# A new order table, searched with a price for each change of TensorE's tile shape

## The chip, the cores and the metric

The kernel runs on one core of one Trainium2 chip. The metric is device time in microseconds (us) of one execution. Five engines matter: PE (TensorE, matrix multiply), DVE (VectorE), ACT (ScalarE), POOL (GpSimd) and SP (SyncE, which here only issues DMAs). Each engine works through its own queue in order and waits on semaphores for the others.

## The reference

Two independent layers, whose outputs are put side by side (L = 2048, D = 576):

```
A:  K = 2 Re( sum_n C[d,n] exp(A[d,n] dt[d] l) )      (d = 576, n = 128, l = 2048)
    y = causal convolution of u with K (by FFT of length 4096) + u * D_skip
B:  q, k, v = x @ wqkv          (32 heads of 18)
    phi(z) = [softmax(z w_phi), softmax(-z w_phi)]
    o = phi(q) (phi(k)^T v) / (phi(q) sum phi(k) + 1e-6);   out = o @ wo
out = concat(A, B)              (2048 x 1152, float32)
```

## The kernel before, in words

The function `body` doesn't issue instructions. It records 2902 operations through `Plan.op` (engine, planned cost, dependences, buffers, and for PE a tile shape `mode`), and `Plan.run` then issues them in the order of the table `ORDER`. The table is the only thing that sets the order on every queue. An entry is the number of an operation; `*` says that the operation goes to its second engine (a copy listed as ACT may go to DVE, a product listed as POOL may go to DVE, or the other way round), `/3` names the buffer slot that a tile gets (8 PSUM slots `ps`, 14 large ones, 19 row ones, 7 small ones), and `+12` puts twelve dummy matmuls on zeros (line 227) ahead of a PE operation.

```
            x, *slots = x.split("/")
            x, _, fill = x.partition("+")
            second, k = x.endswith("*"), int(x.rstrip("*"))
```

The work falls into units. The helpers `mm` (line 447), `copy` (452 to 457) and `tt` (462 and 466) issue most of it, so lines alone say little; the tiles' names do:

- **fold**: w_phi is multiplied into the weights, `ps<-fT,e`; the result is split in a high and a low half, `wh` and `wl`.
- **key** (16 tiles of 128 tokens): three products of 14 matmuls each with `wh` and `wl`; the two softmaxes (`small`, `e`: on DVE maxima, minima and `e<-ps,small`; then `e<-small,e`, the exponential on ACT (592), pair sums `o<-e` on POOL (595), and the scaling `e<-e,small` and `v<-v,small`); then the state phi(k)^T v, `ps<-e,v`, 32 small products in 128x32 tiles. The sixteenth of these ends the first stage of the kernel.
- **query** (16 tiles): a product, softmax, transposes (697), `ps<-kvb,fT`, transposes (726), the output product, `ot`.
- **u** (16): the first step of u's transform, `ps<-kb,w`, in 32x64 tiles, copied to `zi`.
- **group** (18, two halves each): the kernel K by powers. Phases are added on POOL (899), cosines and sines come from ACT (909 to 917), exponents from PE (`ps<-sel,mg`) and ACT (933), the factors `E` and `cs` from DVE (944, 948, 950) with some on POOL, and `ps<-E,cs` on PE in 128x32 tiles. The last of its 36 halves ends the second stage.
- **kfirst**, **product**, **last**: the other steps of the transform: `ps<-ks,w` in 32x128, `ps<-ub,ff` in 64x32 and `ps<-kb,ff`, `ps<-ac,ff` in 32x32, `ps<-zi,w` in 128x64 tiles, with copies out of PSUM to `zi`, `us`, `zo`, `yo`, 288 wide.

Of the 486 PE operations 336 use the whole 128x128 array, 150 a smaller tile shape.

Of the kernel before, what the change touches and what calls it, by code (L numbers as in the profile page):

```python
# [277 lines left out]
0/0 2 1 3 261/0 4/1 153/2 234/3 374/4 33 396/5 12/1 72/6 288/7 19/8 1363 1362 40/2 46/0 375/3  # L278
1360 5/4 369/9 1361 26/5 376 1249/10 1329 377* 13+26/0 15 266/11 16 35/1 20/2 1368 1367 1369/12 1371 1370
1372 14/3 17 22 21/4 38 34/5 1373 18 41 1374 1379 36 23 1167 50/13 1250*/14 47 42 1331/6  # L280
48 1375 1364 39 1376 24 1365/0 1377 1518 25 1366 7+32/6 1378 1380 1381/15 1519 10 11 6/7 8
1289/16 9 27+2/0 1332/7 37 1382 1333/8 29 1251 1383 28/3 31 379+2/2 212/17 1384 30 1349/18 1330 1385 43/9
267/10 1252/1/4/6/7/11 131/4 32 1386 1523 1256 1387 1388 268* 269* 1253 1255 1516 382/0 380/5 1353/8 1199/12 239/1 1334
1335 1179/15 397 1291/10 383 1517 51/12 1341/1 1389 1390 1475/0 1336 271/0 1290 482 384/13 1309/14 1239/11 1337 1524
52* 1342 213/0 53 1476 1525/16 385 1292/3/7/1/6/1 1477 1168 1338 272/2 1296 1293 1254 1258/0 347/10 1257 386 1478
1344 1295 44 1527 270/0 388*/1 387 1479 55/6 274/2 1294 1339 278 389 1297 56/3 132/4 45 1351/13 1480
57/4 58/3 59 1535 60/5 275 1354 276/2 390 277 1340 1520 1481 1201/8 381/1 1200 391/12 1521/1 62 1699
1522 61 63 73 1350 1343 64*/4 65 1526 1345 158/18 279 214* 240/6 273/7 215 218/5 74 398 133*
392/5 280*/6 1346 393/0 66 67/17 1347 1348 289 1298 241* 54/1 394 1484 1482 1352 1202/6/0/3/4/8 1528 1209/12 242
223/1 217/1 1205 68/3 1204 1206 290 281* 1483 395 399 69/4 245/2 224 225/9 70* 1203 1529 1391/0 1392  # L290
1434/1 1435 348/11 1207 219/3 1241/8 221 1485 1436 1698 75* 1437 1530 1531 220 222 235 1438 1439 1490/0/10/7
1532 483 1533 1700 236* 282 1503/4/1/12 1488/7 1505/6 251/2 1486/5 1491 49/1 401/13 1548/1 246/3 71 1489 1219/1 226*/5
250 216/2 1493 283/17 1494 1208 1487 1506 1534 76 400 1440 227 1299/16 243/3 1492 1547 284/6 134 228
285/0 252/5 1279/6 244/0 263 229/4 1536 1701 1705 1537/17 1210/5 262 1504 1495 1355 1496 137/5 230/3 1538 104/4
286* 1539 455/17 1441 1442 1240* 248 231/4 1501/3 428/11 1540 287 143/1 1510 1356 247 1541 1497/2/13/0 154 232
1542 378/4 136/7 349* 253/5 1511 350 1702 1502 1498 249 135/5 138/4 254 1319/10 1509 1706 1507 237 255
1508 1512/0 1543 233 142 140 155 144/8 139 1242/3/6/4/5/6 256/8 351/6 291* 402/7 1513 1499 238 141 1246 320/3
429/10 1544 1545 1245 1244* 1243 1248 292 1269/7 1447/5/3/1 352/4 159/12 145*/6 1357 1443 1444 430* 257/3 293/8 258/2
431 353/3 1546 1221/11 146 1220 355/5 1707/1 356 1549/0 432/7 1247 1550 1551 1445/7 354/6 1552 1500 1553 359
1554 1717 358 147 1446 370 361/4 357/4 1709 1449/2 435/4 371 1451 1448 1450 360 1514 1515 362 105/9  # L300
1555 160* 1454 434/6 1452 363 1211 148/12 1453 1212/7/3/0/2/2 1455 1358 321/6 1214* 161 1456/5 450/5 364/18 452 1216
# [12 lines left out]
1421/4 1729/0 469/2 1415/3 1425 1422 470 184 1424 1169/15 421 426 1429 191/5 1128/4 1416 1601/0/7/5 1724 1730 113/3
471 1428 1427 472/2 1417 208 1603/2 1426 1430/4 1899 1604 112 1725 114/11 422 111/7 1884 473/5 1418 322
196 1600 1726 474/4 197 128 323 324/13 110/6 198 294/1 1889/2 1605/3 1610 1727 1728 1431 207 199*/2 200*
295* 1602 1813/1 475* 1642/5/3/9 480 1606 115 1611 127 1432 1643 1607 1609 1814 325/7 476 201 1815 1644/2
116 1608 328/1 1645 1646/0 427 202/3 1647 1612/3 1649 117 481 1613 1614 118/0 1816 119 1652 327/6 1650
1651 120 1817 1615 1818 1616 1433 1648 1618/0/2/3/4/12 344/1 329 296 78/5 203/6 1621 1819 326/6 204/2 121/12 330/7
297/14 298/5 1620 205* 122/5 210 331 1891 1622 1619* 123/4 1820 1822 1623/1 206 315/8 342 1624/3/7/2/4/2 79* 99/3  # L320
124* 343 299/0 1890 1170/12 1892 332 125* 334/3 301/0 333 129 1628* 1823 300/6 1627 1821 302 316 303/6
304 1626 1617 335 1636/2/4/5/7/13 336 305 1893 306 80* 307*/6 308 1270/2 81/15 1653/0/12/1 337/9 1625 1629 1638 1637*
130 1640 1301/18 338/2 1630/2/3/4/7/3 309 1772/0 1773 1774 1639 1654 1641 317 1655 1633 1828/5/9/11 1632* 1775 1824/6 1826/4
1631* 339/5 1634 1829 1832 1776 83/3 1831 1825 1777 1827 1833 1635 1830 1894 534/0 1778 100 82/7 1779
1834 310/9 89/1 340 345 84/2 1895 311/4 85 1281*/9 1781 341 312/3 1656 88 90/2 86 1780 1280* 1271*
# [12 lines left out]
1678 1668/0 1675 1669 1677 1140/9 1175 1177 1674 1302+13/7/2/6/1/3 632 1909 1679/0 1686 633/10 1141/6 538 1303 1142 1693
1306 1305 1304 1687/7 1143 634/2 1308 1746/1/8/11 1683/6 1911/1 1144 1688 1692 1307 1145+2/2/8 1684 539 1691 1680 1147/4/16
# [811 lines left out]
```

## Time and profile before

| | |
|---|---|
| median of 3 runs | 540.7 us (539.54 to 542.01) |
| span of the profiled execution | 538.2 us |
| PE busy | 519.2 us |
| DVE busy | 455.0 us |
| ACT busy | 412.1 us |
| POOL busy | 332.1 us |

The results give no time of the profiled execution of its own beside the span, which counts from its first to its last instruction; the median of the runs is 2.5 us above it. Sums below are made in the span.

### The profile page before, as it was taken

To read this page: it belongs to the slowest core of one execution; us is meant where nothing else is said; L and a number is where in the kernel's file an instruction comes from. 1 tells how busy PE (TensorE), PEld (TensorE's weight loads), DVE (VectorE), ACT (ScalarE), POOL (GpSimd) and SP (SyncE) were. 2 spreads that over 40 slices of the span, in tenths; PEclk is the share of its full clock that TensorE was granted. 3 is DMA by queue.
4 is the path that set the end of the run, shared out by engine and by line. 5 is a ranking of instruction groups with operands and counts; after the bars stand their busy time and mean duration, and the time that the engine had idled before them with its cause. 6 is when DMAs were issued, how large, how long until landed. Compare 5 with 4: busy or idle time off the path is not lost.

```text
span 538.2 us, 19714 instructions
## 1 busy us (share of the span) xinstructions
PE 519.2 (96%) x8198; PEld 435.3 (81%) x8198; DVE 455.0 (85%) x992; ACT 412.1 (77%) x728; POOL 332.1 (62%) x379
## 2 busy tenths in 40 slices
PE   7899999999999889999998999999999999999996
PEld 6799988999988678798896877876788896777985
DVE  3799998899998888999996999898968669868563
ACT  4699989899879988989898788899796455554432
POOL 1568899977978875975584579768365245223310
PEclk9899999999999999999999999999999999999999
DMA  8898893633426495575397756797466876997687
GB/s 261 290 314 241 282 344 121 213 84 136 142 91 200 120 321 155 146 188 190 94 265 267 247 178 203 229 302 229 149 226 207 253 220 212 306 292 225 203 299 207
DMA packets 77496, 116.41 MB, mean 216 GB/s; under 512 B 9187, under 2 KB 54371, under 8 KB 77407
## 3 DMA queue, kind: packets, MB, share of 16 engines
q1 hardware_dynamic: 77406, 115.16, 67.8%
q8 instruction: 64, 1.05, 0.8%
q14 instruction: 26, 0.20, 0.1%
HBM read 65.87 MB, written 49.26 MB: 214 GB/s over the span
## 4 chain that ended last, share of the span: by engine, by line
PE 73%; DVE 8%; ACT 6%; POOL 6%; DMA 4%; issue 2%; SPq 0%; POOLq 0%; ACTq 0%; DVEq 0%
PE ps L447 68%; PE ps L697 3%; POOL cs L899 3%; DMA ub<-in_u_dram 1%; DMA e<-in_wqT_dram 1%; DMA e<-in_wkT_dram 1%; PE ps L726 1%; DVE cs L944 1%; POOL e L462 1%; DVE ac L466 1%; DMA ff<-in_ff_dram 1%; ACT e L592 1%; POOL E L462 1%; DVE small L584 1%; DVE e L466 1%
## 5 line engine op out<-in xcount | busy, mean ns | idle before, releaser
L447 PE MATMUL ps<-wh,x 128*128 128x288 f32 (+2 forms) x1008 | 242.0, 320 | 2.4 <-ACT wh L513 1.9
L447 PEld LDWEIGHTS ps<-wh,x 128*128 128x128 f32 x1008 | 174.2, 189 | 14.2 <-ACT wh L513 2.2
L447 PE MATMUL ps<-wl,x 128*128 128x288 f32 (+2 forms) x560 | 176.1, 315 | 0.3 <-DVE wl L514 0.3
L447 PEld LDWEIGHTS ps<-wl,x 128*128 128x128 f32 x560 | 106.0, 189 | 1.4 <-DVE wl L514 0.6
L899 POOL TENSOR_TENSOR cs<-cs,pi 128x64 int32<-128x64 int32 (+4 forms) x90 | 92.0, 1022 | 6.1
L595 POOL TENSOR_TENSOR o<-e 128x576 f32<-128x576 f32 x32 | 42.6, 1334 | 33.2 <-ACT e L592 25.7
L462 POOL TENSOR_TENSOR E<-v,cs 128x512 f32<-128x512 f32 x30 | 38.1, 1290 | 28.4 <-ACT v L940 28.3
L466 DVE TENSOR_TENSOR ac<-us,ps 128x576 f32<-128x576 f32 x64 | 44.8, 746 | 6.6 <-PE ps L447 4.8
L462 POOL TENSOR_TENSOR e<-e,small 128x576 f32<-128x576 f32 x31 | 36.7, 1183 | 14.9 <-DVE small L462 13.9
L933 ACT ACTIVATE ps<-ps 128x512 f32<-128x512 f32 x72 | 41.7, 592 | 5.2 <-PE ps L447 4.8
L944 DVE TENSOR_TENSOR cs<-ps,cs 128x1024 f32<-128x1024 f32 x36 | 43.7, 1214 | 2.1 <-ACT ps L933 1.7
L447 PEld LDWEIGHTS ps<-E,cs 128*32 128x32 f32 x2304 | 34.2, 110 | 13.7 <-issue 7.8
L447 PEld LDWEIGHTS ps<-kvb,fT 126*128 126x128 f32 (+1 forms) x320 | 39.1, 189 | 6.5 <-issue 1.9
L447 PE MATMUL ps<-sel,mg 128*128 128x512 f32 x108 | 41.8, 442 | 1.4 <-ACT zi L452 0.4
L447 PE MATMUL ps<-E,cs 128*32 128x64 f32 x2304 | 40.0, 221 | 2.7 <-issue 0.8
L447 PE MATMUL ps<-kvb,fT 126*128 126x133 f32 (+1 forms) x320 | 42.4, 280 | 0.0
L917 ACT ACTIVATE cs<-cs,hp 128x1024 f32<-128x1024 f32 x36 | 40.6, 1143 | 0.0
L592 ACT ACTIVATE e<-e 128x1152 f32<-128x1152 f32 x32 | 37.4, 1168 | 3.6 <-POOL e L462 3.4
L452 ACT ACTIVATE zi<-ps 128x288 f32<-128x288 f32 x91 | 32.2, 414 | 10.2 <-PE ps L447 10.0
L462 POOL TENSOR_TENSOR e<-small,e 128x576 f32<-128x576 f32 x26 | 31.4, 1206 | 10.9 <-DVE e L466 3.9
L909 ACT ACTIVATE cs<-cs 128x2048 f32<-128x2048 int32 x18 | 34.5, 1919 | 3.7 <-POOL cs L899 3.7
L916 ACT ACTIVATE cs<-cs 128x1024 f32<-128x1024 int32 x36 | 36.8, 1054 | 0.3
(145 smaller groups left out, 1056.2 us busy)
## 6 DMA issues: line engine op xcount, KB each, us to landing
dram<-zi SPq DMA_DIRECT2D x32, 288.0 KB
xd<-x SPq DMA_DIRECT2D x16, 576.0 KB
x<-xd SPq DMA_DIRECT2D x16, 576.0 KB
dram<-zi SPq DMA_DIRECT2D x16, 576.0 KB
kb<-dram SPq DMA_DIRECT2D x32, 288.0 KB
ub<-dram SPq DMA_DIRECT2D x32, 288.0 KB
dram<-zo SPq DMA_DIRECT2D x32, 288.0 KB
zi<-dram SPq DMA_DIRECT2D x16, 576.0 KB
```

Of the source, the lines that this page charges most:

```text
L447: pe.matmul(o, l, r, start=start, stop=stop, skip_group_check=skip)
L452: op(("act", "dve"), (c_act(n), c_dve(n)), lambda e: act.activation(dst(), src(), AF.Copy) if e == "act" else dve.tensor_copy(dst(), src() ...
L462: op(eng, [c_dve(n[0]) if e == "dve" else c_pool(n[1]) for e in eng], lambda e: (dve if e == "dve" else pool).tensor_tensor(dst(), a(), b( ...
L466: op(eng, c_dve(n) if eng == "dve" else c_pool(n), lambda: e.tensor_tensor(dst(), a(), b(), op=alu), r=r, w=w, with_=with_, lock=eng == "p ...
L592: op("act", c_act(1152) + 40, lambda: act.activation(e.t, e.t, AF.Exp), r=[e], w=[e], table="exp")
L595: op("pool", c_pool(517), lambda: pool.tensor_tensor(pair.t, e.t[:, :, :, 0:9], e.t[:, :, :, 9:18], op=ALU.add), r=[e], w=[pair], lock=True)
L899: op("pool", c_add(4 * n * W), lambda n=n, j=j: pool.tensor_tensor(x()[:, :, :, n:2 * n], x()[:, :, :, 0:n], pi.t[:, j:j + 2, gs].bitcast( ...
L909: op(("act", "dve"), (c_act(n) + 45, c_dve(n)), lambda e: act.activation(cs.t[:, 0], x(), AF.Abs) if e == "act" else dve.scalar_tensor_ten ...
L916: op("act", c_act(64 * W) + 150, lambda at=at: act.activation(at(1), at(1).bitcast(I32), AF.Sin, scale=TURN), r=[cs], w=[sine], with_=[cs] ...
L917: op("act", c_act(64 * W) + 225, lambda at=at: act.activation(at(0), at(0), AF.Sin, scale=-TURN, bias=hp.t), r=[cs, hp, sine], w=[both], w ...
L933: op("act", c_act(512) + 12, lambda: act.activation(ps.t, ps.t, AF.Exp), r=[ps], w=[ps], table="exp")
L944: op("dve", c_dve(64 * W), lambda: dve.tensor_tensor(F(), both(M.t), F(), op=ALU.mult), r=[M, ready], w=[long], with_=[cs])
```

## The change

Only the table `ORDER` is replaced (one line longer; line numbers behind it rise by one, so that 447 becomes 448). Operations, buffers and arithmetic are the same.

```diff
 ORDER = """
-0/0 2 1 3 261/0 4/1 153/2 234/3 374/4 33 396/5 12/1 72/6 288/7 19/8 1363 1362 40/2 46/0 375/3
...
+2607 1103 2736 836 1104* 2737 2633 2632 2860/0 2861/3/0/16 2895/7 2896/4/5/18 2853/4 2862 2863 837/0/5 2897* 839/6
...
 """.split()
```

Counted in the two tables, in issue order:

| | before | after |
|---|---|---|
| changes of tile shape between successive PE operations | 209 | 187 |
| of these up to the sixteenth key state product | 50 | 42 |
| up to the last of the 36 group products | 161 | 138 |
| dummy matmuls, ahead of so many operations | 94, 10 | 59, 2 |
| operations on DVE | 992 | 1027 |
| operations on ACT | 686 | 637 |
| operations on POOL | 375 | 389 |
| DMAs on SP | 363 | 363 |

The order on every queue is perturbed from end to end, while the sequence of units stays nearly the same. Two places show what moves.

PE's queue in the key stage, before, around a visit to the small tile shapes (`x_529` and `x_737` are the input tiles of two key tiles, `v_95` and `v_107` the values of two others):

```order
L447 MATMUL ps<-wl,x_529 128x396
L447 MATMUL ps<-E,cs 32x64 x32
L447 MATMUL ps<-kb,w_210 64x288 x8
L447 MATMUL ps<-e,v_95 19x36 x32
L447 MATMUL ps<-e,v_107 19x36 x32
L447 MATMUL ps<-sel,mg 128x512
L447 MATMUL ps<-wh,x_737 128x378
```

The same stretch of PE's queue after (`x_519` and `x_960` are input tiles, `v_85`, `v_701`, `v_720` and `v_396` values of four key tiles):

```order
L448 MATMUL ps<-wl,x_519 128x396
L448 MATMUL ps<-e,v_85 19x36 x32
L448 MATMUL ps<-E,cs 32x64 x64
L448 MATMUL ps<-e,v_701 19x36 x32
L448 MATMUL ps<-e,v_720 19x36 x32
L448 MATMUL ps<-e,v_396 19x36 x32
L448 MATMUL ps<-kb,w_256 64x288 x8
L448 MATMUL ps<-wh,x_960 128x378
```

Six operations in 128x32 tiles now stand in one visit; before, this visit held three of them, split by one in 32x64.

POOL's queue before, at the first softmaxes of the key tiles (`e<-small,e` forms the second exponent, `cs<-cs,pi` adds phases for a group):

```order
L899 TENSOR_TENSOR cs<-cs,pi 128x64x8
L462 TENSOR_TENSOR e<-small,e 128x576
L899 TENSOR_TENSOR cs<-cs,pi 128x64x16
L595 TENSOR_TENSOR o<-e 128x576
L462 TENSOR_TENSOR e<-small,e 128x576
L462 TENSOR_TENSOR x_432<-zo,x_432 64x128
```

DVE's queue after, at the first softmaxes of the key tiles:

```order
L467 TENSOR_TENSOR e<-ps,small 128x378
L463 TENSOR_TENSOR kb<-ub 128x288
L463 TENSOR_TENSOR small<-small 128x32
L463 TENSOR_TENSOR kb<-ub 128x288
L463 TENSOR_TENSOR e<-small,e 128x576
L463 TENSOR_TENSOR x_519<-zo,x_519 128x512
L463 TENSOR_TENSOR e<-small,e 128x576
```

Two of the second exponents that stood on POOL now stand on DVE. Over the whole table DVE gains 35 copies of 128x288 out of PSUM from ACT (u 5, kfirst 5, product 10 into `us` and 4 into `zo`, last 5, query 6) and 14 smaller copies; from POOL it gains one `e<-small,e` (four more in the key stage, three fewer in the query stage), three `e<-e,small` and two `v<-v,small`, and it gives up seven `ac<-ac`, three `E<-v,cs` and eleven of the tiny `small<-small`.

Counted along DVE's queue, the last DVE operation that the sixteenth key state product depends on is the 359th before and the 380th after; for the last group product it is the 808th before and the 827th after.

More of the change, by code (lines that the diff above doesn't have):

```diff
@@ new lines @@
+249 1540 1501/5 1502 1507 228 229/13 1503/4 1504 1510 219/7 236 1493 230/0 136/1 246/2 1700 1705 231/1 254 1506 1508
+76 1511 1541 1542 347/9 348/8 1356 140/5 255 1509 1543 232 1357 233 1544 1441 1547/1 1442 153 1443 234 287* 1358 1240
+263 237* 243/5 349* 1211/11 350 139 1207 1545 256/9 428/13 1512/3/5/9 154 1497/4 1498 1499 1500 141/12 143 142 144
+429/13 430* 1219/18 238 292 1221/4 1701 1706 1297 1708 1717 1707/5 431* 400 126/7 145*/1 1208 1242/2/7/5/4/11 1245
+1710 1513* 1246* 146 1243 1514 1244 1444 257/5 353/1 1248 370*/13 1546 1549/1 358/1 1447/7/3/2 1220 1448 359 1445/2
@@ new lines @@
+166 1228 1473 443 168/12 1562/5/2/3 365/4 1299/16 1474 1227 1394 1395 1459 1575/2/7/13 1229/9 1180/6 1579/7 1580 1396
+1563 1570 1702 1564/3 1582 1569 1583 1397 164/4 169 170 1565 444 1699 1576 1567 445/1 408/1 446/1 1560/7 366/5 171
+1577/5 1578 1398 1561 172*/3 1711 1566 1568 173 181 407/6 406/4 413/3 367 368 104/3 456/6 165/3 1585 457* 372* 373
+105/8 447/4 174 458 448* 1261/18 412 1581 1584 1571/2 449 414/1 410 409 1399 411 1400 207/5 1586/5 453 175/13 1587*
+415/4 425 185/8 186/10 182 454 187* 1703/0 1401 1406/4/7/13 1404/3 1408/1 1588 482 1712 1405 1713 1714 176/3 177/1
@@ new lines @@
+121/1 299/7 316 329 330/5 206 1821 298/2 300/3 122/3 210 332 123/5 1627 331 333 334/4 304/2 124 335* 305 306/0 301 129
+336 1617 1636/1/7/4/5/13 1638 302 1637 303 1640 1653/2/12/8 125 1270/1 307*/5 308* 1301/13 1628* 1629 317* 1639* 1641
+337/8 1892 309 338/5 339/2 1884 1772/1 1773 1630/1/3/7/6/6 1632* 1774 1634 1279/12 1824/5/10/9 1775 1654 1655 1825
+340* 1656 1776 1777 1828/4 297/15 1830 1633 1829 1831 1826/6 1827 1834 1631 1833 83/3 100* 310/8 341 88/5
+1262/1/5/7/2/11 1264* 1266* 1894 89 1635 1271* 311/4 312/3 427 1832 82/6 85 1319/18 313 1265* 1263 1267 1268 84/2 1778
@@ new lines @@
+1134 1175* 1907 1908 1909 1135 1137/5 1173* 1136 623/7 1739 628 627 626/13 629 1138 630/2 631 1012/2 1014/4 1668/5
+1670/0 1015 1741 1673 1676 1675 1013/7 1327 1177 1669 1674 1139 1140/16 1302/1/6/4/3/0 1671 1678 1141/3 632
+1683/5/11/5 1684 1306 633/13 1178 1305 1017 1142 1143 1144 538 539 1677 634/3 1016/10 1685/3 1686 1693 1692 1746/4/4/1
+1747 1304 1018 1679/0 635 1020/5 636 1680 2038 1681 637 1019 1682 1145/2/13 1303 1146 1147/6/16 1149/1/0 1148 1687/3
+1688 497 1744/2 540/3 1151/6 1745 1150 1689 541 1742/1 1154/0 1743 642/5/13 643 638/7/0 639 1690 1691 1694/3 640/7/16
@@ new lines @@
+1857 2046 1919 1862/0/1/4/6/11 1864* 1027 1858* 2037 2055 2041/0 2042 1912 1969/2/4/3 2049 2048 1860* 2219 1230/17
+2050 2051 1920 2052 1866 1307 2053 656/3 658* 1855 659 2054 1028/5/2 1865 1863* 1867 2056 1032/7/14 2057/4 1033 2058
+1166 1190/7 2059 2060 2061 2062 1970/10 2218 1973* 701/1 705 706 2220 1965/7 1029* 1030/0/18 1966 1861 1031 708/5
+1967/4 1968 857/3 1972* 1921 1868/5/0/2/6/10 1870 1869 707 1971 709 862/2 861 1872* 1922 1974 863/11 1037/1 1034/7
+1231* 1871 1923 1874/3/5/0/6/0 1038/3 1975 1976/2/2/1 1310* 2222 1035/4 1036/2 1875* 2063 2064 1039 1040/1/3 2065
@@ new lines @@
+1940 2469/17 1924/6 1048 718/3/2 716/7/9 1925 1945 1930 719 935/2 721 725/5 726/4 717 722/1 2001 1935/6 723/0 724/2
+727 2002 2003 1946* 1950/4 870 871 939 940 941 872/5/9 873 1951* 728/1/7 1952 1953 729/0 2470/18 874/2/1 875* 2066
+2069/1 2070 730 2478/13 2449/16 2472/4/5/3/0/2/10 2474* 2475* 2004 2473 2071 1936 878/2 2477/14 731 732 1937
+2479/7/3/5/4/13/8 2221 1938 2535/0 2480 2226 2481 894/9 2476 2483 876/0/9 2005 2482 879/3 2072 2073 880/10 2074 2075
+2491/4 2078 2076 734/6 736*/2 877* 733/3 2223/1 2537/5 735 2227/13 2229 2543/15 2228 2231 2484/2/5/4/7/14/7 2536/12
@@ new lines @@
+2170* 2464* 2500/9 2499/1 910 2501/2/7/4/1/2/4 2465 2257 2466* 2162/0 2163 2505 544/6 2260 2502 2468 2504 2463* 2467
+2258 2503 546/5 2168 547 548/5 2559/5 968/2 2150/7/3/4/1/8 2152* 2151* 970* 2740/12 971 2153* 2169* 2154 2173/0/12/7
+2174* 2149/3 2259 2175 2261 2156/3/1/6/5/9 2160 2264/4/13/1 2558/18 2265 2158* 2176 2159* 911/2/3 912* 596
+2506/5/1/7/0/7/1 2157* 2509* 2262/2 2510 2508 2266/3 2512 2507* 915/0/4 2263 2271 2272 2268 2267/6 2428/1/7/6/5/9/14
+2429* 2333/0 2408/0 2334 2335 2431* 2511 2432* 913/3/15 914* 2336 2337 545/4 549 916 2402/11 2338 550 2339 551 2340
@@ new lines @@
+928/0 609/3 610/7 2688/15 558 2417 2298 2299 2300 930*/9 2560/5/6/7/4/11/0 2563 2561* 2566/8 2301 2564* 2446 2351*
+2352* 2355/0 559 560/5/5 2363/4/9/1 2562* 561 2361/7 2362 2411 2364/17 2366* 2367* 2413 607 2356* 2414 2415 2357 2358
+562/6/18 563 2369 929/1 2418/5/3/2/0/4/16 931 2368 2419 2420* 2421* 2359/6 2360 564/7/6 565 2365 2565/3
+2567/5/1/4/3/0/11 738/6 739/2 2571 2307/3/5/8 2570 2569 2422 2568 2308/17 2311 611/6/0 2661/10 612/10 613 2370/4 2371*
+2372 2373 2177/0 2572/5/1/3/7/11/7 2574* 2302 2573* 566/6 2318/5/0/11 2322/1 2178 2576 2320/7 2179 741/5 2305/4 2180
@@ new lines @@
+2381 2397* 2391 2791/4/2/5 2395* 677/7/13 2398 764/1 765/5 2792* 2793 761/6 766/9 2396 762/0 763 2399 1060 1061
+1062/16 2389 678 2393 2794 2795 779/2 784 783 785 786*/0 787 767/4/6 768/3 769 1063/3 1064 2832/11 679/1/2 770 771
+974/7 978/5 681/4/9 979 682* 980/4 973/2 975 1065 2823 976 680 686/4 687/3 688/9 788 683/7 977 2833/2/4/16 789/17 2834
+790/3 1066 2695/7 2694/15 2696/6/1/3/0/2/5 684/4 685 689/7/5 981/2 982 983 2701 690/11 984/9 2796 2824 2702 691 692
+772/4 2703 774/18 2704 2835 1069/7/11 2836 1070 2660/2 1067/0/7 1068 693 2697 2698 2663/5/4/2/3/15/5 2667 2664* 2665
@@ new lines @@
+2669/17 2666 2668/13 2670/1/0/6/7/6/0 1071/5/4 2699 2700 1072 2671 1073/4 2705/1/5/2/3/13/17 2672 2709 2804/1 2706
+2675 985/4 2676 986 987 791 1089/7 792 2707 2837 2673 793 2838 2812/6/0/7 2580/6 2813 2805/1/3/9 2814 2677 2581/10
+2708 2806* 2815 2807 2808 2741/2/0/7/5/5/16 2742 1076/6 2747/15 2744 2743 1074/3 1075/0 2746/14 2748/7/1/2/3/1/9
+796/4/4 2674 1077/0 1078 2745 2753 2678 694/6 797 2754 2749 2711/2 2755 696/16 2679/7/3/4/2/14/15 2682 2710 2683
+2636/12 2816 2750 2582/1/5/0/6/5/13 2817 794/2/2 2751* 2681* 2752 2586 2809 2680* 2584 795 2756* 2757/7/3/4/6/6/10
@@ new lines @@
+2761 2583* 2587/17 2585* 2758 2588/11 2589/1/5/0/2/0/6 2598 2635/7 2597 2599 2759 2760 988 695/6 2590 697 2591 2592
+2593 2594 2637/0/2/4/3/13/11 2641 2685 798/5/5 799 2595* 2596* 800/6 801/2 2765/1 2639 2600* 2638* 2684 2640 803/4
+804/0 2601/2/5/3/1/2/14 2605 2602 2762 2603 989/0/4 802/5 2642/17 2604 805 990 2643/15 2644/6/7/4/1/0/6 2645 806/5/2
+2763 2766/7 2646 807/12 808 2647 2650 2648 773/3 809 775 810 2764/12 2767/5/7/6/0/13/5 2768 2771 2649 2651* 2652
+2772/6 2773/3 698 2770* 2774/2/3/1/4/3/11 2779 2780 2781 2769 2776 991/5/11 992 2775 2714/10 811/7 813/5 2712/15
@@ new lines @@
+2713/17 2810 776 2653/3/4/5/1/3/6 2655 2782 2654 2715/2/6/0/7/13/16 2717* 2718 993/3/18 2719 2716* 995/4 2657* 996/0
+997/4 2721/1 2720/7 2722/1/2/7/6/4/0 2728 994 998/3 2608/9 2656 2727 2724 999/0 2777 2778 2617/8 2723 2729 1000 2730
+812/4 814 2783/2/7/6/5/16/11 2787* 2609/10 2784 2785* 2610/17 2786 2725 2611/3/1/0/4/13/18 2615* 2726 2616/1
+2618/7/6/5/2/3/11 2613 2612 1001/4/1 1002/12 2614 2620 816/6 818/3 2619 2624 2731/0/7/6/2/13/4 2735 2732 2621 2734
+2622 2733 1003 2623 2625* 2789 2658 2788 822/0 817/4 2626* 820 819 2627/7/6/0/5/16/18 2606 1090/2 2629 1004 1005 2631*
@@ L424 @@
+1117 1118/2/6 1119/6 1010 1120 2854/4/7/4 2855* 2856 1121 1122 2875/0/3/9 2881/7 2876 2857 2868/7/2/0 2858 2877 2869
+2889/3/6/16 2901 2878 2880 2890* 2891 2879 2847/0/2/13 2870 2871 2848 2872 2882/6/4/5 2873 2883 1124/2 2859 2849 851/4
+2892 2894 2884 2885 2886 852/6 2850 2893 853* 2851 2887 1126*/0 854 1123/0 2852 1125 1127
 """.split()
```

228 lines of the change are left out of this document (83 added, 145 removed).

## The prediction

> **What bounds the kernel now.** I read the busy times of the page first, then the stages, then the waits.
>
> ```profile
> span 538.2 us, 19714 instructions
> PE 519.2 (96%) x8198; PEld 435.3 (81%) x8198; DVE 455.0 (85%) x992; ACT 412.1 (77%) x728; POOL 332.1 (62%) x379
> ```
>
> PE is busy for 96% of the span, so what PE does and waits for is the time. But 85% for DVE is a mean over unlike stages. I cut the span at two landmarks that both orders have, the sixteenth key state product and the last group product, and look at the stages between them (timeline of PE, then busy time by window: length, PE, PEld, DVE, ACT, POOL, granted clock, DMA share, GB/s):
>
> ```profile
> 195.85 0.75 PE L447 MATMUL ps<-e,v 128*19 128x36 f32 x64
> 418.46 1.10 PE L447 MATMUL ps<-E,cs 128*32 128x64 f32 x64
> ...
> 0.00:20.00 20.00, 14.70 (x117) 12.41 (x118) 10.32 (x27) 11.85 (x24) 3.40 (x15) 0.97 0.82 258
> 20.00:80.00 60.00, 59.81 (x733) 55.29 (x732) 57.07 (x113) 52.48 (x85) 49.06 (x56) 0.98 0.91 298
> 0.00:195.80 195.80, 187.66 (x2811) 167.89 (x2811) 172.41 (x363) 165.48 (x267) 150.32 (x189) 0.98 0.64 208
> 195.80:418.50 222.70, 216.36 (x3852) 175.00 (x3853) 200.71 (x450) 191.56 (x323) 149.46 (x157) 1.00 0.67 207
> 418.50:538.20 119.70, 115.18 (x1543) 92.44 (x1541) 81.87 (x182) 55.08 (x139) 32.34 (x35) 1.00 0.79 247
> 183.00:193.00 10.00, 8.04 (x178) 5.58 (x179) 8.21 (x18) 7.70 (x21) 6.59 (x10) 0.83 0.95 289
> ```
>
> In the first stage DVE works 172.4 of 195.8 us. Of its 23.4 idle, 9.7 lie in the first 20 us, where the first data are still landing; between 20 and 80 us it idles 2.9 of 60, or 4.9%. In the second stage it works 200.7 of 222.7. Only in the third, at 81.9 of 119.7, does it have time to spare. For the first 418 us the kernel thus has two nearly full engines, PE and DVE, and an order that keeps each just ahead of the other. PE's idle time has no single cause (waits of PE):
>
> ```profile
> PE ps L447 <- ACT wh L513: 1.9, 1, 1.9
> PE ps L227 <- DVE ident L480: 1.7, 1, 1.7
> PE ps L447 <- DMA ff<-in_ff_dram: 1.5, 1, 1.5
> ```
>
> **The change part by part.** *Changes of tile shape, 209 to 187.* Their price shows in the timeline of PE, as the time from the start of one operation to the next:
>
> ```profile
> 58.49 1.31 PE L447 MATMUL ps<-e,v 128*19 128x36 f32 x128
> 59.73 0.44 PE L447 MATMUL ps<-wh,x 128*128 128x378 f32 x1
> ...
> 133.32 1.10 PE L447 MATMUL ps<-E,cs 128*32 128x64 f32 x64
> 134.24 0.76 PE L447 MATMUL ps<-e,v 128*19 128x36 f32 x64
> 134.93 0.44 PE L447 MATMUL ps<-wh,x 128*128 128x378 f32 x1
> ...
> 137.99 1.10 PE L447 MATMUL ps<-E,cs 128*32 128x64 f32 x64
> 139.03 0.45 PE L447 MATMUL ps<-wh,x 128*128 128x396 f32 x1
> ```
>
> A group product followed by the same 128x32 shape takes 134.24 - 133.32 = 0.92 us, followed by the full array 139.03 - 137.99 = 1.04: the change costs 0.12. For the key state product two in a row take 1.24 and one before a change 0.69, so one without is 0.55 and the change 0.14. I take 0.12 for every kind, though only leaving 128x32 is shown. 22 fewer are worth 2.6 us of PE: eight in the first stage (1.0), fifteen in the second (1.8), and one more in the third (0.1 lost). The Trainium skill, TensorEngine Tiling (Array Packing), Key Properties, says that changing the tiling mode, not the tile, drains TensorE; these rows agree, and give the drain its price.
>
> *Dummy matmuls.* The start keeps 59 for 58 plus 4, which I cost at nothing. The other 32, in the middle, go:
>
> ```profile
> L227 PE MATMUL ps<-ident,zero 32*64 32x256 bf16 x13 | 1.6, 269 | 0.0
> L227 PE MATMUL ps<-ident,zero 32*32 32x256 bf16 x9 | 1.3, 270 | 0.0
> L227 PE MATMUL ps<-ident,zero 64*32 64x256 bf16 x7 | 0.9, 270 | 0.0
> 221.14 1.04 PE L447 MATMUL ps<-E,cs 128*32 128x64 f32 x60 [0.32 <-DVE cs L944]
> ```
>
> These 29 of the 32 take 3.8 us, which is about the most that their loss gives. Right behind the thirteen (218.6 to 220.0 us) PE waits for DVE all the same, so I take 0. What they may have kept up is the clock, a rival below.
>
> *Work that changes engine.* By busy time over count of these rows of DVE:
>
> ```profile
> L452 DVE COPY zi<-ps 128x288 f32<-128x288 f32 x37 | 15.3, 444 | 4.0 <-PE ps L447 4.0
> L452 DVE COPY zo<-ps 128x288 f32<-128x288 f32 x18 | 7.8, 452 | 4.0 <-PE ps L447 3.9
> L452 DVE COPY us<-ps 128x288 f32<-128x288 f32 x16 | 6.8, 442 | 1.6 <-PE ps L447 1.5
> L452 DVE COPY ks<-ps 128x128 f32<-128x128 f32 x7 | 2.0, 286 | 1.5 <-PE ps L447 1.5
> L462 DVE TENSOR_TENSOR e<-small,e 128x576 f32<-128x576 f32 x6 | 5.6, 933 | 0.1
> L462 DVE TENSOR_TENSOR e<-e,small 128x576 f32<-128x576 f32 x1 | 0.7, 749 | 0.0
> L462 DVE TENSOR_TENSOR v<-v,small 128x608 f32<-128x608 f32 x2 | 2.1, 1048 | 0.0
> L462 DVE TENSOR_TENSOR kb<-ub 128x288 f32<-128x288 f32 x23 | 13.3, 588 | 1.3 <-PE ps L447 1.3
> L462 DVE TENSOR_TENSOR ac<-ac 128x288 f32<-128x288 f32 x15 | 7.9, 560 | 0.1
> L462 DVE TENSOR_TENSOR E<-v,cs 128x512 f32<-128x512 f32 x6 | 4.8, 806 | 0.1
> L462 DVE TENSOR_TENSOR small<-small 128x32 f32<-128x32 f32 x35 | 11.0, 320 | 0.2
> L948 DVE TENSOR_TENSOR E<-ps,cs 128x512 f32<-128x512 f32 x36 | 24.6, 682 | 1.2 <-ACT ps L933 1.2
> ```
>
> DVE gains 35 wide copies at 29.9/71 = 0.42 (14.8 us), 14 smaller ones at 0.3 (4.2), one `e<-small,e` (0.9), three `e<-e,small` (2.1), two `v<-v,small` (2.1), and loses seven `ac` (3.7), three `E` (2.4) and eleven `small` (3.5): 14.5 us more, 455 to some 470. ACT sheds as many copies, which costs nothing there.
>
> What counts is where. Of the 21 DVE operations that the sixteenth key state product now waits for beyond the 359 of before, four are `e<-small,e` (3.7), two `e<-e,small` (1.4), two `v<-v,small` (2.1), four factors `E` (2.7), three on `ks` (0.9), two `kb` (1.2), and four others net about 1.3: 13.3 us more DVE work ahead of a product that PE's own queue reaches with 1.0 us less work. So the first stage asks 172.4 + 13.3 = 185.7 of DVE. With the idle time of the first 20 us alone it would last 185.7 + 9.7 = 195.4 (0.4 less than now), with all of today's idle time 209.1 (13.3 more). Between these ends the nearest row is the stretch in which DVE is pressed hardest, 20 to 80 us: 20 + (185.7 - 10.3)/0.951 = 204.4, so 8.6 more. This I take; PE, queued behind, waits for the difference, and everything behind it with it.
>
> The second stage has two DVE operations fewer (19 more by its end against 21 more by its start): seven `E` (4.8), three `kb` (1.7), two `e<-small,e` (1.9) and seven `small` (2.2) move out of it, fourteen wide copies (5.9) in, and three others net about 1.7 in: 3 us less. Together with 1.8 on PE that gives 4.8 off. The ends are nothing, where the waits stay, and 8.1, where PE's busy 216.4 less 1.8 is the whole of the stage. In series the two engines' savings add, as their waits for each other alternate here, so I take 4.8.
>
> The third stage: some 5 us more on DVE are hidden under its 37.8 idle; were these gone, they would show in full. One shape change more costs 0.1. DMAs keep their number and bytes; SP's queue is reordered with the rest, and its waits in the rows of PE above are 1.5 at most, so 0, between 1.5 less and 1.5 more.
>
> Sum: 538.2 + 8.6 - 4.8 + 0.1 = 542.1 of span. With the 2.5 between the span and the median, 540.7 becomes 544.6.
>
> **The rivals.**
>
> *DVE closes its gaps (faster).* Once DVE is the later engine, its inputs lie ready, and the 13.7 idle after the first 20 us shrink to the 0.4 with which the first stage lasts as long as now. For it: 49 copies leave ACT, for which DVE waits today. Against it: no long stretch shows DVE above 95%. If the first stage comes out at 195.4, the sum is 538.2 - 0.4 - 4.8 + 0.1 = 533.1, 535.6 with the 2.5. It decides from a DVE idle share of 2.6% behind the first 20 us downwards: there the first stage lasts 20 + 175.4/0.974 = 200.1, 4.3 more, and the sum is 537.8, 0.4 below now.
>
> *It cancels (same).* The first stage costs about 5, as between the two cases, and the second returns it: 541.
>
> *The clock (slower still).* Without the 32 dummies PE may fall to half clock. In the row of 183 to 193 us PE was busy for 8.0 of 10 us and the granted clock was 0.83, which is 1.7 us lost. If DVE now makes PE wait in the places without dummies, two or three such losses add 3.4 to 5.1 to my sum: 548 to 550. Against it: the second stage as a whole shows 1.00. The Trainium skill, TensorE: Matmul & The Clock Gate, "Why this matters for your kernels", asks for no idle gaps above about 3 us between bursts; the row disagrees in that PE was idle for only 2.0 us in all there.
>
> *The change doesn't do what it says.* 187 against 209 are a count of the table, so this is out; only the price per change can be smaller, and at 0 my sum rises by 1.8.
>
> **How the numbers follow.** My case, DVE as the later engine, 0.42; the clock on top of it 0.06; cancelling 0.23; gaps closed 0.29. A measurement of this kernel can tell about 0.5%, 2.7 us, from no change. So slower 0.48, same 0.23, faster 0.29. The predicted time is 544.6. The lowest sum of the bounds is 538.2 - 0.4 - 8.1 = 529.7, 532 with the 2.5; the highest is 538.2 + 13.3 + 0.1, 554. I leave out the last of each side: 533 to 553. My case alone: 542 to 550.
>
> **What would show it.** Right: DVE busy about 470; the sixteenth key state product at about 204 us, with DVE idle near 5% from 20 us to there and PE idle on releasers named DVE; the second stage at about 218 us; about 120 after the last group product. Wrong: the sixteenth product at 196 or earlier (gaps closed), a clock under 0.95 in a window behind 195 us (the clock), or a shape change that costs no 0.12 in PE's timeline. What would upset all of it is a transfer or a chain through ACT and POOL that the new order makes late, which no row of before shows.

## The result, and the profile after

The kernel after takes 559.09 us (median of 4 runs, 556.95 to 563.02) where the kernel before takes 541.14 (4 runs, 539.54 to 542.01): a ratio of 1.0326, 95% interval 1.0272 to 1.0381. It is 3.3% slower, and above the range of 533 to 553. The profiled execution took 563.02 us, the slowest of the four; its span is read here against the 538.2 of before, so the loss in the span, 23.0 us, is larger than the 18 us between the medians. The head of its page, and its waits of PE (engine, line, who was waited for: us in total, times, longest):

```profile
span 561.2 us, 19716 instructions
PE 522.3 (93%) x8163; PEld 437.8 (78%) x8163; DVE 467.2 (83%) x1027; ACT 400.6 (71%) x680; POOL 331.5 (59%) x393
q8 instruction: 64, 1.05, 0.7%
...
PE ps L448 <- issue: 18.1, 10, 3.0
PE ps L448 <- ACT zi L453: 2.9, 2, 2.0
PE ps L227 <- DVE wl L515: 2.1, 1, 2.1
```

Of the 23.0 us of span, 19.9 are PE's idle time (561.2 - 522.3 = 38.9 against 19.0) and 3.1 its busy time. The first row of the waits names no engine: "issue" means that PE stood still and nothing in the profile held it. It stands for 18.1 us in ten stops; eight of them, 15.8 us, lie in group and key state products, two among other small products. Before has the same row, far down its list, at 1.1 us:

```profile
PE ps L447 <- issue: 1.1, 2, 0.8
```

The stops fall inside operations, where no semaphore is waited for. The timeline of PE in the kernel after, around the two earliest:

```profile
75.80 0.74 PE L448 MATMUL ps<-E,cs 128*32 128x64 f32 x38
79.22 0.31 PE L448 MATMUL ps<-E,cs 128*32 128x64 f32 x5 [2.68 <-issue]
79.35 1.51 PE L448 MATMUL ps<-e,v 128*19 128x36 f32 x122
82.77 1.28 PE L448 MATMUL ps<-e,v 128*19 128x36 f32 x70 [1.92 <-issue]
```

A group product stops five matmuls before its end, two key state products follow, and 122 matmuls further on the next stop comes. Counting all instructions of PE from the start (its 16,326 weight loads and matmuls and the 204 semaphore and drain instructions between them, 16,530 in all), these two stops stand before instructions 1218 and 1473, the others before 3009, 4033, 5058, 5569, 6081, 8386, 12225 and 13506. Divided by 256, each leaves 193 or 194. And 256 fits the packets of the page's queue q8, "instruction": 64 of 16,384 bytes (1.05 MB) for 16,530 instructions, about 258 to each. In the trace each of the ten stops ends 2.2 to 2.8 us after such a packet starts. So PE stops where a packet of its own program has not come. The packets of this trace are 3.3 us or more apart. The table after, which saves shape changes by putting group products (0.92 us for 128 instructions) beside key state products (0.55 us), lets PE work through 256 instructions in less.

The stages (busy time by window: length, PE, PEld, DVE, ACT, POOL, granted clock, DMA share, GB/s), cut at the sixteenth key state product and the last group product:

```profile
0.00:215.10 215.10, 192.40 (x2803) 173.65 (x2803) 179.44 (x382) 163.12 (x262) 134.78 (x176) 0.95 0.56 178
215.10:438.50 223.40, 214.98 (x3819) 172.87 (x3823) 200.94 (x450) 189.49 (x305) 154.72 (x168) 0.98 0.64 204
438.50:561.20 122.70, 114.96 (x1557) 91.26 (x1545) 86.84 (x197) 48.02 (x114) 42.01 (x51) 0.99 0.85 266
60.00:80.00 20.00, 16.90 (x345) 16.01 (x346) 16.72 (x32) 15.70 (x23) 10.72 (x17) 1.00 0.43 144
80.00:100.00 20.00, 18.08 (x255) 16.12 (x244) 15.64 (x40) 12.15 (x18) 9.81 (x13) 0.83 0.34 103
80.10:86.90 6.80, 4.88 (x147) 3.75 (x133) 5.41 (x18) 2.09 (x6) 2.30 (x5) 0.50 0.02 5
203.00:206.40 3.40, 3.40 (x123) 2.44 (x115) 1.09 (x2) 0.85 (x3) 1.35 (x2) 0.50 0.92 261
```

19.3 us of the loss lie in the first stage, with 11.8 us of the stops; 0.7 in the second (4.7 us of stops), 3.0 in the third (1.6). In the two rows of 20 us DVE, which was to be the later engine, idles 3.3 and 4.4 us. The mean granted clock of the whole span is 0.973, before 0.993. The last two rows show where it fell: of six stretches at half clock between 25 us and the end of PE's work, 23.8 us in all, four (17.0 us) begin within 1.4 us of the end of a stop. Before has one such stretch, of 3.4 us.

### The profile page after: what moved, and what is told of

It reads as the page before. It is cut to its first block, busy times and chain, and to the rows that moved or that the text cites. A ratio compares the mean times of both kernels' runs of the same rounds, so it can differ in the third digit from the quotient of the medians.

```text
span 561.2 us, 19716 instructions
## 1 busy us (share of the span) xinstructions
PE 522.3 (93%) x8163; PEld 437.8 (78%) x8163; DVE 467.2 (83%) x1027; ACT 400.6 (71%) x680; POOL 331.5 (59%) x393
## 3 DMA queue, kind: packets, MB, share of 16 engines
q8 instruction: 64, 1.05, 0.7%
## 5 line engine op out<-in xcount | busy, mean ns | idle before, releaser
L900 POOL TENSOR_TENSOR cs<-cs,pi 128x64 int32<-128x64 int32 (+4 forms) x90 | 90.7, 1007 | 5.7
L463 POOL TENSOR_TENSOR E<-v,cs 128x512 f32<-128x512 f32 x33 | 42.1, 1294 | 15.3 <-ACT v L941 15.0
L448 PEld LDWEIGHTS ps<-E,cs 128*32 128x32 f32 x2304 | 35.5, 112 | 19.3 <-issue 14.9
L453 ACT ACTIVATE zi<-ps 128x288 f32<-128x288 f32 x81 | 29.4, 411 | 19.0 <-PE ps L448 18.1
L882 POOL TENSOR_TENSOR pi<-pi 128x192 int32<-128x192 int32 (+1 forms) x42 | 20.6, 507 | 35.7 <-DVE pi L878 21.1
L448 PE MATMUL ps<-kvb,fT 126*128 126x133 f32 (+1 forms) x320 | 41.1, 278 | 0.0
L463 POOL TENSOR_TENSOR e<-e,small 128x576 f32<-128x576 f32 x28 | 33.1, 1184 | 6.5 <-DVE small L463 4.1
```

The costliest lines, as they stand in the source:

```text
L448: pe.matmul(o, l, r, start=start, stop=stop, skip_group_check=skip)
L453: op(("act", "dve"), (c_act(n), c_dve(n)), lambda e: act.activation(dst(), src(), AF.Copy) if e == "act" else dve.tensor_copy(dst(), src() ...
L463: op(eng, [c_dve(n[0]) if e == "dve" else c_pool(n[1]) for e in eng], lambda e: (dve if e == "dve" else pool).tensor_tensor(dst(), a(), b( ...
L882: op("pool", 200 + 1.37 * n * BW, lambda: pool.tensor_tensor(ip(o, n), ip(x, n), ip(y, n), op=ALU.add), r=[pi], w=[pi], lock=True)
L900: op("pool", c_add(4 * n * W), lambda n=n, j=j: pool.tensor_tensor(x()[:, :, :, n:2 * n], x()[:, :, :, 0:n], pi.t[:, j:j + 2, gs].bitcast( ...
```

## The experiments

Theory F: the packets of instructions hold PE back. Theory D, the prediction's: DVE is the later engine.

**Same order, half the instructions in the small products.** This pair decides. In both kernels the group products and the key state products are issued as half as many matmuls of double width.

```diff
-            for d in range(DG):
+            for d in range(0, DG, 2):
...
-                        mm(ps.t[32 * m:32 * m + 32, d, :], cs.t[:, r, c0 + m * DG + d, 0:32], E[r].t[:, m * DG + d, :], r == 0, r == 1, True)
+                        mm(ps.t[32 * m:32 * m + 32, d:d + 2, :], cs.t[:, r, c0 + m * DG + d, 0:32], E[r].t[:, m * DG + d:m * DG + d + 2, :], r == 0, r == 1, True)
...
-            for h in range(H):
+            for h in range(16):
...
-                mm(kvt.t[32 * j:32 * j + 19, g, :], v1.t[:, h, :], e.t[:, :, h, :], t == 0 and g == 0, t == NT - 1, True)
+                mm(kvt.t[32 * j:32 * j + 19, 2 * g:2 * g + 2, :], v1.t[:, h, :], e.t[:, :, 2 * h:2 * h + 2, :], t == 0 and g == 0, t == NT - 1, True)
```

> The kernel before, in which each group product and each key state product is made of half as many matmuls, each over twice as many columns (128 for 64, 72 for 36); half of the products are thereby left out and the others written over their places, while operands, places and dependences stay. The order and the engines are those of before; TensorE has about the same work, with 1,664 matmuls and as many weight loads fewer. It is the partner of the next kernel. Theory F: before has 1.1 us of stops without a wait, so little is gained, 537 to 541. Theory D: 538 to 542.

> The same in the kernel after: its order and its engines, with half as many matmuls of twice the columns in each group product and key state product. Theory F (fetching of instructions): 256 instructions of PE now take 3.5 us or more nearly everywhere, the 18 us of stops without a wait fall under 2, the sixteenth key state product comes at 196 to 202 us instead of 215, and the time is 537 to 544, within 1% of its partner. Theory D (DVE is the later engine in this order, whatever PE does): the sixteenth product comes at 204 or later and the time is 550 or more, over 2% above its partner. If the clock that was lost in after (0.973 granted instead of 0.993) comes from the stops, it is back above 0.985; if it comes from the missing dummy matmuls, it stays near 0.973.

Before with wide matmuls: 538.28 us (ratio to before 0.9921, 0.9891 to 0.9952). After with wide matmuls: 539.74 us (0.9941, 0.9918 to 0.9964). The 18 us between the two orders are gone; what is left, 0.3%, is inside the intervals. Head and waits of the second kernel, then the stages of the first and of the second (each with a row from 20 us to the end of the first stage):

```profile
span 535.9 us, 16388 instructions
PE 511.3 (95%) x6499; PEld 426.2 (80%) x6499; DVE 467.5 (87%) x1027; ACT 400.0 (75%) x680; POOL 332.2 (62%) x393
...
PE ps L448 <- issue: 1.4, 2, 1.3
```

```profile
20.00:198.20 178.20, 172.77 (x1836) 153.33 (x1836) 164.01 (x339) 153.40 (x243) 150.98 (x176) 0.98 0.62 203
0.00:198.20 198.20, 187.87 (x1951) 165.81 (x1953) 173.92 (x364) 165.54 (x267) 154.33 (x191) 0.98 0.64 208
198.20:418.10 219.90, 214.29 (x3083) 171.46 (x3082) 199.20 (x447) 191.42 (x323) 146.40 (x155) 1.00 0.66 207
418.10:538.10 120.00, 115.10 (x1511) 92.45 (x1509) 82.02 (x182) 55.16 (x139) 32.39 (x35) 1.00 0.79 247
```

```profile
20.00:201.60 181.60, 171.65 (x1812) 152.42 (x1811) 170.20 (x354) 150.83 (x239) 133.43 (x167) 0.98 0.56 180
0.00:201.60 201.60, 187.10 (x1943) 166.90 (x1944) 181.07 (x382) 162.75 (x262) 135.21 (x176) 0.98 0.59 189
201.60:415.40 213.80, 209.60 (x3051) 168.21 (x3055) 199.53 (x450) 189.31 (x305) 154.87 (x168) 1.00 0.68 212
415.40:535.90 120.50, 114.63 (x1517) 91.08 (x1509) 86.91 (x197) 47.97 (x114) 42.10 (x51) 0.99 0.87 271
```

With the stops down to 1.4 us (none in the partner), the order after costs 3.4 us in the first stage (201.6 against 198.2), gains 6.1 in the second and loses 0.5 in the third. The stages are read from one execution of each, 539.88 and 537.70 us, while the medians differ by 1.5 us the other way, so they are good to a few us only. DVE has the same 467 us to do as in the kernel after, so D falls. The granted clock is 0.992, so the clock that after lost went with the stops. PE's work is not what changed: its busy time times the granted clock is 508 us in the kernel after and 507 here. The queue now brings 51 packets, for 13,202 instructions.

**The packets' edges moved, in the kernel before.**

```diff
-            n = min(256, t.shape[1])
+            n = min(64 if fill == 90 else 256, t.shape[1])
...
-... 377* 13+26/0 15 ...
+... 377* 13+90/0 15 ...
```

> The kernel before with 64 dummy matmuls more at its start (90 in the place of 26, each 64 columns wide instead of 256, so that this fill takes about as long in all). All that follows is the same, but each of PE's later instructions stands 128 places further back, so the edges of the packets of 256 fall elsewhere. Theory F: by the durations of the rows the packets that take less than 3.5 us now fall short by 11.1 us in sum instead of 4.4, so the stops without a wait rise from 1 us to some 5 to 8, and the time by 4 to 8 us, to 545 to 549. Theory D, and any theory by which only the order matters: no change, 539 to 542.5.

554.06 us, a ratio of 1.0203 (1.0164 to 1.0243). F had the direction and about half the size: 11.5 us over the 542.53 that before took beside it, for 4 to 8. The work behind the dummies is the same in the same order on every engine, and five stops inside key state and group products appear, all in the first stage. The waits, one stop, and the first stage:

```profile
PE ps L447 <- issue: 10.7, 5, 3.1
...
104.02 0.47 PE L447 MATMUL ps<-e,v 128*19 128x36 f32 x30
107.57 0.76 PE L447 MATMUL ps<-e,v 128*19 128x36 f32 x34 [3.08 <-issue]
...
0.00:214.00 214.00, 194.44 (x2879) 175.18 (x2882) 174.11 (x363) 165.37 (x267) 150.98 (x189) 0.96 0.59 191
```

The stage is 18.1 us longer than before's, with 10.7 us of stops. The rest was not split by a run of its own: the granted clock is 0.96 for 0.98 (some 4 us of 214), and the first product with `wh` starts at 19.54 us instead of 18.07, as the eight matmuls right behind the thin dummies took 2.04 us for 1.13.

A second shift, by 32 instructions, was to remove the stops:

```diff
-            n = min(256, t.shape[1])
+            n = min(160 if fill == 42 else 256, t.shape[1])
...
-... 377* 13+26/0 15 ...
+... 377* 13+42/0 15 ...
```

> The kernel before with 16 dummy matmuls more at its start (42, each 160 columns wide, in the place of 26 with 256), so that PE's later instructions stand 32 places further back. Theory F: the packets of 256 that take less than 3.5 us now fall short by 1.3 us in sum instead of 4.4, most of which lies behind other waits, so the stops without a wait, 1.1 us in before, go and 0 to 2 us are gained: 539 to 542. If the edges of the packets did not matter and the 64 dummies of the other shift had cost their 11 us by themselves, a quarter of that would show here: 544 to 545.

544.18 us, a ratio of 1.0046 (1.0015 to 1.0077): a miss, at the value that was to speak against the edges. The trace tells why it doesn't. PE was even 0.6 us early at its first product with `wh` (17.47 us), so the dummies cost nothing there, but the stops rose from 1.1 to 6.5 us. The longest lies among wide matmuls, where the durations alone show no short packet:

```profile
PE ps L447 <- issue: 6.5, 5, 2.5
...
99.37 0.51 PE L447 MATMUL ps<-wh,x 128*128 128x378 f32 x2
102.40 0.44 PE L447 MATMUL ps<-wl,x 128*128 128x378 f32 x1 [2.52 <-issue]
...
98.00:100.00 2.00, 1.88 (x11) 1.56 (x10) 1.97 (x6) 1.06 (x2) 1.84 (x4) 1.00 1.01 396
```

The packet that PE lacked there started at 100.19 us, 4.5 us after PE had passed the edge before (95.72); over the whole run the middle value of this delay is 1.4 us. From 92 to 100 us the DMA engines were busy for 0.83 to 1.01 of the time. This suggests that a packet also waits for the data transfers ahead of it, which is tested by itself below.

**The packets alone.** TensorE on zeros, first without other work, then beside loads:

```diff
+        small(ps("n64"), e, 512, 64)
...
+        small(ps("n36"), e, 512, 36, 19)
...
+        small(ps("n128"), e, 512, 128)
...
+        for n in (32, 64, 96, 128):
+            small(ps("n64"), e, n, 64)
...
```

> TensorE alone, all other work left out: rows of 512 matmuls on zeros, each of which gives two weight loads and two matmuls. First 32 x 64 columns as in a group product, then 19 x 36 as in a key state product, then 32 x 128, then the full array with 288 columns; short rows of 32, 64, 96 and 128 matmuls among wide ones; at the end 32 x 64 again while the output is written by DMA. Theory F: 256 instructions cannot follow one another in less than about 3.5 us, so the first two rows take about 8 x 3.5 = 28 us each, though at the pace inside a product they would take 14.7 and 8.8; the third takes 28 to 30, the fourth 70 or more without a stop. Short rows up to about 64 matmuls run at their own pace, and longer ones stop once. With DMA traffic the interval is the same or longer. Against F: the rows take 14.7 and 8.8 us, and the stops of the large kernels have another cause.

```profile
13.87 2.77 PE L33 MATMUL n<-z,a 128*32 128x64 f32 x183
17.80 1.99 PE L33 MATMUL n<-z,a 128*32 128x64 f32 x128 [1.16 <-issue]
21.53 1.99 PE L33 MATMUL n<-z,a 128*32 128x64 f32 x128 [1.74 <-issue]
...
54.88 1.27 PE L33 MATMUL n<-z,a 128*19 128x36 f32 x128 [2.02 <-issue]
58.61 2.12 PE L33 MATMUL n<-z,a 128*19 128x36 f32 x128 [2.46 <-issue]
...
86.41 28.31 PE L33 MATMUL n<-z,a 128*32 128x128 f32 x1024
124.45 248.48 PE L49 MATMUL n<-z,a 128*128 128x288 f32 x1024
389.61 1.99 PE L33 MATMUL n<-z,a 128*32 128x64 f32 x128
422.77 2.88 PE L33 MATMUL n<-z,a 128*32 128x64 f32 x191
426.74 0.22 PE L33 MATMUL n<-z,a 128*32 128x64 f32 x1 [1.09 <-issue]
```

After every 128 matmuls with their 128 weight loads PE stops, and starts again 3.45 to 3.73 us after its last start (21.53 - 17.80 = 3.73), or 4.01 once, whether the work between takes 2.0 us or 1.3. The row of 64 columns takes 26.7 us instead of 14.7 (16 times the 0.92 of a group product), that of 36 columns 25.3 instead of 8.8 (16 times 0.55), and 128 columns fill the interval without a stop (28.3). Of the short rows 128 matmul records (64 calls) pass unhindered and 192 stop once. Against the expectation, nothing here tells of DMA traffic: the output's transfers had ended before the last row began. So a second kernel of the kind, with loads:

```diff
+        for k in range(64):
+            sp.dma_start(x[:, k], u[128 * (k % 16):128 * (k % 16) + 128])
```

> TensorE alone on zeros, as in the first kernel of that kind, whose transfers had ended before its last row began: a row of 512 matmuls of 32 x 64 columns without DMA, then the same row and one of 32 x 128 columns while 64 loads of 295 KB each run (18.9 MB, by the 320 GB/s of the busiest slices some 59 us). Theory Q (the packets of instructions queue behind data transfers): in the rows under load the packets are more than 4 us apart and the stops longer than the 1.2 to 1.7 us of the row without load, so the second row takes 30 us or more, and the third has stops, which it did not have alone. Against Q: 26 to 27 us, and 28 us without a stop, as without load.

```profile
71.60 1.99 PE L33 MATMUL n<-z,a 128*32 128x64 f32 x128 [1.74 <-issue]
75.05 1.99 PE L33 MATMUL n<-z,a 128*32 128x64 f32 x128 [1.46 <-issue]
...
98.08 2.65 PE L56 MATMUL busy<-z,b 128*32 128x64 f32 x128 [3.75 <-issue]
102.63 3.59 PE L56 MATMUL busy<-z,b 128*32 128x64 f32 x128 [1.90 <-issue]
108.83 3.12 PE L56 MATMUL busy<-z,b 128*32 128x64 f32 x128 [2.61 <-issue]
...
60.00:80.00 20.00, 11.17 (x728) 10.41 (x731) 0.00 (x0) 0.00 (x0) 0.00 (x0) 1.00 0.02 5
100.00:120.00 20.00, 11.23 (x420) 10.44 (x415) 0.00 (x0) 0.00 (x0) 0.00 (x0) 0.59 1.02 373
```

Beside the loads the row takes 41.4 us instead of 27.1, with stops of 17.6 us instead of 11.2: packets come every 4.4 to 6.4 us. The row of 128 columns takes 34.7 with two stops, 1.61 and 2.50, where it took 28.3 without. The granted clock fell as well (0.59 in the last row above), but a slower PE needs its next packet later, which shortens a stop; and in the first kernel the row of 36 columns ran mostly at a clock of 0.50 while its packets still came every 3.5 to 4.1 us. Q holds. The Trainium skill, Runtime: NRT & Kernel Launch, Instruction fetch mechanics, says that instructions come in 16 KiB blocks of 256, that the next is fetched while the present one runs, and that crossing a block is mostly hidden. The size agrees with the packets of 16,384 bytes; in these runs the fetch was hidden only where 256 instructions last 3.5 us or more, and longer beside transfers.

**Repairs that failed.** With DVE's queue and all others left alone, twelve PE operations were moved by more than two places so that no packet was short. At one of the places, with PE's entries of the table alone and without their slots (1571 and 1586 are group products, 454 a key state product, the others wide products):

```diff
-1571 1586 454 1406 1404 1408 461 460
+1571 1586 1406 1404 1408 461 454 460
```

> The order of the kernel after, in which some PE operations alone (twelve by more than two places) stand elsewhere, so that small matmuls (group products and key state products) are spread among wide ones; the order on every other engine and the choice of engines are those of after. Theory F (fetching of instructions): PE's instructions come in packets of 256, and PE stops where it has worked through 256 of them in less than about 3.5 us, as in the kernel after ten times, 18.1 us in all. In this order no 256 instructions take less than 3.5 us by the durations of the rows, so the groups ended by no wait fall from 18 to under 2 us, and the time from 559 to about 540 to 545, although there are six changes of tile shape more than in after. Theory D (DVE has become the later engine, as predicted): DVE has the same operations in the same order, so the time stays at 553 or more, and what PE no longer waits for instructions it waits for DVE.

> The order in which PE's small products were spread (566.6 us), with the half as many and twice as wide matmuls of the pair of kernels above (half of the products are left out), so that no fetch can hold PE back. Theory M (moving the twelve PE operations made the engines that wait for them late, and this took the place of the stops): the waits for DVE and ACT stay and the time is 555 or more. Theory R (the stops that were left, 3.7 us, set it all off): 538 to 545.

566.6 us (ratio to before 1.0443, 1.0403 to 1.0483), and with the wide matmuls 560.78 (1.0373, 1.033 to 1.0417). F missed the first: the stops fell to 3.7 us, not under 2, and the time rose. What D said for it came true, 553 or more with PE waiting for DVE: PE's waits for DVE and ACT in the first stage rose from 8.0 to 17.9 us. But DVE's queue is that of the kernel after, where the wide matmuls brought 539.74. The second kernel here, with no stop at all, shows that the moves alone cost it (M): about 21 us over the same wide matmuls in the order after. These are its longest waits:

```profile
PE ps L446 <- ACT zi L451: 8.2, 6, 2.0
PE ps L446 <- DVE E L465: 4.4, 3, 2.3
PE ps L446 <- DVE cs L943: 2.7, 2, 2.5
```

**The engines exchanged.** Each order with the other's choice of engines (205 entries gain or lose their `*`):

```diff
-... 376 ... 377* ... 1250*/14 ... 1255 ... 1295 ... 65 ...
+... 376* ... 377 ... 1250/14 ... 1255* ... 1295* ... 65* ...
```

> The order of the kernel before, with the engines that after chooses for the operations that may run on either of two (DVE some 467 us busy instead of 455). PE's instructions stay those of before. Theory D: 13 us more work on DVE in the first stage cost 5 to 9 us, so 546 to 550. Theory F: PE's instructions are as in before, so 540 to 543, with PE's stops without a wait at about 1 to 2 us.

> The order of the kernel after, with the engines that before chooses (DVE some 455 us busy instead of 467). PE's instructions stay those of after. Theory D: DVE is relieved of what made it late, so 549 to 554. Theory F: PE's stops without a wait stay at 15 to 19 us, so 556 to 562.

570.28 us (1.0527, 1.0474 to 1.0581) and 608.22 (1.1202, 1.1163 to 1.124): far outside all that was expected. The stops were 4.6 and 14.2 us, for the 1 to 2 and 15 to 19 of F, so most of the loss lies elsewhere. An order and its choice of engines thus belong together; the likely reason, that each choice sets who is behind whom in a queue, was not tested. So these two runs don't settle D; the pair with wide matmuls does.

**The dummies.**

```diff
-            n = min(256, t.shape[1])
+            n = min(256 if (rows, cols) == (128, 128) else 1, t.shape[1])
```

> The kernel before, with its 32 dummy matmuls in the middle one column wide instead of 256: they stay in their places, so that no instruction moves, but do no work. Theory P (the prediction): they cost nothing and gain nothing, 538 to 542. Theory C (they keep up the clock, and after lost 11 us by leaving them out): the granted clock falls from 0.993 to 0.98 or less, and the time rises to 545 or more.

541.32 us, a ratio of 0.998 (0.9954 to 1.0006), clock 0.995. The edit reached 29 of the 32, 1.4 us of PE instead of 3.8; the three in full-array tiles kept their width. These 29 neither cost anything that shows nor hold up the clock. No kernel here that computes the whole reference beats before.

## Why the prediction was wrong, by its own steps

- **What failed** is the step *Changes of tile shape*. It counted what putting like shapes together saves, and put the cost of a run of small products at nothing. The small products enter it at 0.92 and 0.55 us, but, as TensorE alone showed, two of them in a row (128 matmuls with their weight loads) did not take less than 3.45 us once the packet at hand was used up. The stops are 17.0 us more than before's (18.1 - 1.1), and the 17.0 us at half clock behind four of them cost up to 8.5 more. Without the stops nothing is left of the loss. The step was signed wrong in its sum: 2.6 us of gain for 17 of loss and more. The part on what would upset all of it names a late transfer that no row of before shows; it was one that no queue of the kernel issues, and before's waits did hold its row, at 1.1 us.
- **The saving itself** is borne out by the pair of wide kernels, as an estimate. Behind the first 20 us PE is 6.3 us less busy in the second (495.9 for 502.2). The middle dummies are some 4.2 of that, which leaves about 2.1, for 2.6 predicted.
- **DVE as the later engine** (+8.6): 3.4 between the wide kernels. DVE's work ahead of the sixteenth product was mis-sized, 13.3 more predicted and 7.2 measured (181.07 for 173.92). Its idle share behind 20 us is 6.3% there, so the 5% taken from the tightest stretch was about right, and the rival in which it falls below 2.6% did not come. In the kernel after the sixteenth product came at 215.1 us, later than the 204 foretold, but with DVE idle for 35.7 us of it.
- **The second stage** (-4.8): 6.1 less between the wide kernels. In the kernel after, 3.6 us more of stops and a clock of 0.98 for 1.00 stand against it; the stage came out 0.7 longer.
- **The third** (+0.1): 0.5 between the wide kernels, 3.0 in the kernel after with 1.6 of stops.
- **The clock** (a rival at 548 to 550): it did fall, but for another reason. The prediction gave the missing dummies as its cause, and 29 of the 32 were shown to do nothing; with the stops gone it is 0.992. The kernel after spends 20.4 us more at half clock than before, up to 10 us lost as an estimate, where the rival had 3.4 to 5.1.
- Without stops *it cancels* would have been the case: 538.3 and 539.7 with wide matmuls.

## What to carry to other kernels

Small matmuls have a price that their duration does not show: count instructions, and where 256 of PE's (weight loads too) take less than about 3.5 us in a row, as measured here, expect a stop, more so beside heavy transfers. A row "<- issue" in the waits of PE, with stops inside an operation and at a fixed remainder of 256, is the sign of it. An order that was searched with a price for shape changes alone can cluster just these products, as here, so the search needs the other price as well.

## What the runs showed of the hardware

- In a row of small matmuls without other traffic PE gets 256 instructions every 3.45 to 4.01 us, and 4.4 to 6.4 us beside loads at 373 to 388 GB/s.
- Stops of under 3 us can halve the granted clock. In the row of 36 columns without load, with stops of 1.6 to 2.5 us and PE busy for 1.3 us between the first two, it stood at 0.50:

```profile
58.00:62.00 4.00, 2.12 (x128) 1.96 (x128) 0.00 (x0) 0.00 (x0) 0.00 (x0) 0.50 0.02 4
```

  The rows of 64 columns kept 1.00 with stops of 1.05 to 1.74 us and 2.0 us of work between them. Beside loads, with stops of 1.7 to 2.6 just behind one of 3.75, the clock was 0.59 over 20 us and went back to 1.00 in between. The Trainium skill, TensorE: Matmul & The Clock Gate, "Why this matters for your kernels", asks for no idle gaps above about 3 us; here shorter ones, close together, were enough.
- 64 more, narrower dummies at the start, with the same instructions in the same order behind them, cost 2% of the whole time; a start that was 1.5 us later is in it.
